# One list schedule for all engines in an attention + two-MLP kernel on one core

## The chip, the cores and the metric

One core of one Trainium2 chip. The metric is the device time of one execution in microseconds (us); lower is better. Three runs of the kernel before gave a median of 1007.41 us (1007.06 to 1010.12). The profile is of a further execution.

## What is computed

Three stages in a row, all float32 (cut from the reference):

```python
scores = (q @ k.T) / 8                      # 4 batches x 8 heads, 576 x 576, head 64
scores = where(scores >= max(scores) - tau, scores, -1e9)
x = softmax(scores) @ v                     # -> 2304 tokens x 512
h = x @ w_in                                # 512 -> 1024
s = h * softmax(h); x = layernorm(s) * g_ln @ w_out      # 1024 -> 512
h = x @ w2_in                               # 512 -> 2048
out = softplus(h) @ w2_out                  # 2048 -> 512
```

The weights arrive as 64-bit numbers, so the kernel turns each of them into float32 itself. Each MLP product is made of three matmuls in the fp32r format (high x high, high x low, low x high), for which every operand is split into a high part (a cast) and a low part (a subtraction).

## The kernel before

**Attention.** Two heads make a pair p (16 pairs), and an *item* is one pair with one or two tiles of 128 query rows, some with a *tail* (the last 64 rows of both heads). 36 items hold 80 score groups. `scores` (L177) multiplies the two heads on the two halves of TensorE's rows; VectorE takes the negated maximum (L187), ScalarE the exponential (L188), VectorE masks and sums (L195). The masked rows are transposed on TensorE through the identity (L210, L219, L221, L231), copied by ScalarE (L212, L224, L232), and multiplied with v (`av`, L276). `rinv`, `rgroup` and L279 bring in the reciprocal of the sums. Score tiles s take 4 of the 8 PSUM banks (one buffer for each head), everything else the 4 banks of the tag w.

**First MLP.** Nine *units* of 256 tokens. For each unit `m1_split` (L344, L345), `m1_h` (12 matmuls in a group, L355, 36 groups), `m1_post` (softmax, mean and variance on VectorE and ScalarE, L367 to L381), `m1_tr` (transposes L390, split L394, L395) and `m1_out` (24 matmuls in a group, L403, 36 groups). Its result x2 goes to DRAM (L407).

**Second MLP.** Five blocks, four of 512 tokens and one of 256, with 16 chunks of 128 hidden columns each. `m2_load` reads x2 back, `m2_split` splits it (ScalarE L541, GpSimd L542). For each chunk `m2_h` (12 matmuls, L573), softplus in nine steps of ScalarE and VectorE (L582 to L594), and `m2_y` (12 matmuls, L612; 6 in the last block).

**Weights.** `convert` makes float32 out of the two words of a weight (ScalarE L80, VectorE L81, L82, L84, ScalarE L87) and the low part (L88): on VectorE for the first MLP (8 pieces of 1024 columns), on GpSimd for the second (32 pieces of 512).

**The order of the work.** `attention` is a generator that yields after each half of a score group. The main loop at its foot gives the first MLP 0.6 of a step (PACE) for each step of attention, and advances the weight conversion at the steps listed in PREP. When attention is over, the rest of the first MLP runs with one conversion of w2_in between two of its steps; then the second MLP follows, with one conversion of w2_out for each chunk of its first block. The second MLP's work tiles lie in space that the first MLP gives back.

```python
493    for s, _ in enumerate(attention()):
494        if s in PREP:
495            next(prep, 0)
496        credit += PACE
497        while credit >= 1:
498            credit = credit - 1 if next(stream, False) else 0.0
```

Of the kernel before, what the change touches and what calls it, by code (L numbers as in the profile page):

```python
# [23 lines left out]
PACE = 0.6  # L24
PREP = [1, 2, 4, 5, 7, 8, 9, 11, *range(13, 37, 3)]
EB = 640

# [4 lines left out]

@with_exitstack
def tile_attention_solu_softplus(ctx: ExitStack, tc: tile.TileContext, q, k, v, tau, w_in, w_out, g_ln, w2_in, w2_out, out):
    nc = tc.nc
    PSUM = bass.MemoryType.PSUM
    pe, dve, act, pool, sp = nc.tensor, nc.vector, nc.scalar, nc.gpsimd, nc.sync
# [26 lines left out]
    items = [(b, h, ts, tail) for b, ts, tail in groups for h in range(NPAIR)]  # L64

    nw = [0]

    def bank():
        nw[0] += 1
        return psW.tile([P, 512], F32, tag="w", name=f"w{nw[0]}", bufs=4)  # L70

    w1h = w1.tile([P, 4, FF1], F32R, tag="w1h", name="w1h")
    w1l = w1.tile([P, 4, FF1], F32R, tag="w1l", name="w1l")
    wo1h = wo1.tile([P, 8, DM], F32R, tag="wo1h", name="wo1h")
    wo1l = wo1.tile([P, 8, DM], F32R, tag="wo1l", name="wo1l")

    def convert(raw, hi, lo, w_, post=None, sub=dve, view=lambda x: x):
        lw, hw = raw[:, :, 0], raw[:, :, 1]
        u = w_.bitcast(U32)
        act.activation(out=w_, in_=hw.bitcast(F32), func=AF.Abs, scale=2.0 ** -112)  # L80
        dve.tensor_scalar(out=lw, in0=lw, scalar1=29, scalar2=None, op0=ALU.logical_shift_right)  # L81
        dve.scalar_tensor_tensor(out=u, in0=u, scalar=3, in1=lw, op0=ALU.logical_shift_left, op1=ALU.bitwise_or)  # L82
        yield
        dve.scalar_tensor_tensor(out=u, in0=hw, scalar=0x80000000, in1=u, op0=ALU.bitwise_and, op1=ALU.bitwise_or)  # L84
        if post is not None:
            post(w_)
        act.copy(out=hi, in_=view(w_))  # L87
        sub.tensor_tensor(out=lo, in0=view(w_), in1=f(hi), op=ALU.subtract)  # L88
        yield

    def prep_w1():
        raws = {}

        def load(i):
            r = raws[i] = m1.tile([P, 1024, 2], U32, tag="lh" if i % 2 else "ll", name=f"raw1_{i}")
            c = 2 * (i % 2) if i < 4 else 2 * (i - 4)
            w = w_in[:, 512 * (i // 2):512 * (i // 2) + 512] if i < 4 else w_out
            sp.dma_start(out=r.rearrange("p (c n) t -> p c (n t)", c=2),
                         in_=w[c * P:(c + 2) * P, :].bitcast(U32).rearrange("(c p) e -> p c e", p=P))

        def two(x):
            return x.rearrange("p (c n) -> p c n", c=2)
        load(0)
        load(1)
        yield
        for i in range(8):
            w_ = m1.tile([P, 1024], F32, tag="u", name=f"w1_{i}", bufs=2)
            if i < 4:
                c, n = 2 * (i % 2), 512 * (i // 2)
                yield from convert(raws[i], w1h[:, c:c + 2, n:n + 512], w1l[:, c:c + 2, n:n + 512], w_, view=two)  # L110
            else:
                c = 2 * (i - 4)
                hi, lo = (w[:, c:c + 2, :].rearrange("p c e -> p (c e)") for w in (wo1h, wo1l))

                def post(w_, c=c):
                    for j in range(2):
                        wj = w_[:, j * DM:(j + 1) * DM]
                        dve.tensor_scalar_mul(wj, wj, g_sb[:, c + j:c + j + 1])
                yield from convert(raws[i], hi, lo, w_, post)
            if i + 2 < 8:  # L120
                load(i + 2)


    st = {}

    def load_qk(p):
        z = st[p] = {}
        z["q"] = at.tile([P, S], F32, tag="q", name=f"q{p}", bufs=NPAIR)
        z["k"] = at.tile([P, 640], F32, tag="k", name=f"k{p}", bufs=NPAIR)
        eng = act if p == 0 else sp  # L130
        for h in range(2):
            r = slice(64 * h, 64 * h + 64)
            sp.dma_start(out=z["k"][r, 0:576 + 64 * h], in_=k[p][:, 576 * h:576 + 640 * h])
            eng.dma_start(out=z["q"][r, :], in_=q[p][:, 640 * h:640 * h + 576])

    def load_v(p):
        z = st[p]
        z["v"] = at.tile([P, 640], F32, tag="v", name=f"v{p}", bufs=NPAIR)
        sp.dma_start(out=z["v"], in_=v[p])

    def scale_q(p):
        z = st[p]
        act.activation(out=z["q"], in_=z["q"], func=AF.Copy, scale=0.125)  # L143
# [4 lines left out]
    pend = []  # L148

    class Item:  # L150
        pass

    def begin(n):
        it = Item()
        it.n = n
        it.b, h, it.ts, it.tail = items[n]
        it.p = it.b * NPAIR + h
        it.h = h
        it.nt = len(it.ts)
        it.W = P * it.nt  # L160
        it.E = []
        it.e = {}
        it.sums = at.tile([P, 5], F32, tag="sums", name=f"sums{n}", bufs=3)
        it.rinv = at.tile([P, 5], F32, tag="rinv", name=f"rinv{n}", bufs=3)
        return it

    def scores(it, k_, apart):
        z = st[it.p]
        tail = k_ == it.nt
        i = 4 if tail else it.ts[k_]  # L170
        ps = [psS.tile([P, 2, 512], F32, tag=f"s{h}", name=f"s{it.n}_{k_}_{h}") for h in range(1 if tail else 2)]
        order = [(nh, h) for h in range(2) for nh in range(2)] if apart else [(nh, h) for nh in range(2) for h in range(2)]
        for nh, h in order:
            r, c, m = slice(64 * h, 64 * h + 64), qcol(h, i), 64 if tail else P
            kc = (64 if h == 1 and tail else 0) + 288 * nh
            o = ps[0][r, nh, 0:288] if tail else ps[h][:, nh, 0:288]
            pe.matmul(o, z["q"][r, c:c + m], z["k"][r, kc:kc + 288], start=True, stop=True)  # L177
        if tail:
            it.T = at.tile([P, 640], F32, tag="T", name=f"T{it.n}")
        else:  # L180
            it.E.append(at.tile([P, 1152], F32, tag="E", name=f"E{it.n}_{k_}", bufs=4))
        for h in range(len(ps)):
            s = 2 * k_ + h
            E = it.T[:, 0:576] if tail else it.E[k_][:, 576 * h:576 * h + 576]
            sv = ps[h][:, :, 0:288]
# [14 lines left out]
    def new_eT(it, what):  # L200
        return at.tile([P, 512], F32, tag="eT", name=f"eT{it.n}_{what}", bufs=NET)
# [281 lines left out]
    for p in range(NPAIR):  # L483
        scale_q(p)
# [206 lines left out]
```

## Time and profile before

| | |
|---|---|
| median of 3 runs | 1007.41 us |
| the profiled execution: time / span | 1010.33 us / 1008.5 us |
| TensorE busy / mean granted clock | 948.4 us (94%) / 0.971 |
| VectorE, ScalarE, GpSimd busy | 713.4, 568.9, 75.1 us |
| largest DMA user | q1, 53.99 MB, 17.1% of 16 engines |

Every engine works off its own queue in order, so an instruction that waits holds all that stand behind it on that engine. "Busy" is the time in which an instruction of the engine runs; matmuls overlap, and the granted clock of TensorE stands at 1.2 or 2.4 GHz, so busy time of TensorE is not work at full speed. The span runs from the first to the last instruction; the execution's time has 1.8 us more.

### The profile page before, as it was taken

How to read it: one execution, taken by the hardware profiler on the slowest of the kernel's cores; microseconds unless marked ns; L12 is line 12 of the kernel's file. 1: busy time of each engine (PE TensorE's matmuls, PEld its weight loads, DVE VectorE, ACT ScalarE, POOL GpSimd, SP SyncE). 2: the span in 40 equal slices, each digit the busy share in tenths (PEclk: the TensorE clock that was granted, in tenths of full speed). 3: DMA queues.
4: the chain of work that ended last, by engine and by line, in shares of the span. 5: the costliest groups of instructions: out<-in, count | busy, mean ns of one | idle time of the engine just before them, and what ended most of it. 6: DMA issues, size and time to landing. Idle time of an engine off the chain costs nothing.

```text
span 1008.5 us, 14610 instructions
## 1 busy us (share of the span) xinstructions
PE 948.4 (94%) x5664; PEld 747.2 (74%) x5664; DVE 713.4 (71%) x1387; ACT 568.9 (56%) x1082; POOL 75.1 (7%) x47
## 2 busy tenths in 40 slices
PE   3898999999999999999997699898999999999997
PEld 2666567777677777876886588676888788888896
DVE  5898866766768577676589959976555755665565
ACT  4765666666657567566556546544444444444453
POOL 0000000000000000000033534311001000000000
PEclk8898899999999999999998799998999999999999
DMA  8412200112001220000054533302000100100010
GB/s 220 173 61 79 75 27 12 35 44 78 27 11 36 65 69 15 12 11 6 33 162 141 162 127 103 125 1 84 1 0 22 63 1 1 42 1 0 1 44 21
DMA packets 27125, 55.21 MB, mean 55 GB/s; under 512 B 3248, under 2 KB 12464, under 8 KB 27056
## 3 DMA queue, kind: packets, MB, share of 16 engines
q1 hardware_dynamic: 26896, 53.99, 17.1%
q8 instruction: 44, 0.72, 0.3%
q10 hardware_dynamic: 160, 0.30, 0.1%
q14 instruction: 25, 0.20, 0.1%
HBM read 44.83 MB, written 9.44 MB: 54 GB/s over the span
## 4 chain that ended last, share of the span: by engine, by line
PE 67%; DVE 18%; ACT 8%; issue 3%; DMA 2%; SPq 0%; DVEq 0%; ACTq 0%
PE y L612 12%; PE h L573 12%; PE s L177 10%; PE w L355 9%; PE w L403 8%; PE w L276 7%; PE w L210 5%; DVE u L82 2%; DVE w L584 2%; DVE t L585 2%; DVE w L591 2%; DMA raw<-in_w_in_dram 2%; DVE u L84 2%; DVE w L592 1%; DVE gl L594 1%
## 5 line engine op out<-in xcount | busy, mean ns | idle before, releaser
L177 PE MATMUL s<-k,q 64*128 64x288 f32 (+1 forms) x640 | 135.0, 445 | 16.8 <-ACT q L143 8.9
L187 DVE TENSOR_REDUCE nm<-s 128x1 f32<-128x576 f32 x144 | 104.5, 750 | 43.4 <-PE s L177 43.4
L573 PE MATMUL h<-x2h,w2h 128*128 128x512 f32 (+1 forms) x320 | 119.3, 375 | 8.6 <-ACT x2h L541 7.0
L188 ACT ACTIVATE E<-s,nm 128x576 f32<-128x576 f32 x128 | 92.5, 741 | 52.6 <-DVE nm L187 52.4
L612 PE MATMUL y<-wo2h,gh 128*128 128x512 f32 x288 | 114.6, 398 | 7.5 <-ACT gh L593 4.3
L573 PE MATMUL h<-x2l,w2h 128*128 128x512 f32 (+1 forms) x320 | 118.8, 371 | 0.8 <-POOL x2l L542 0.8
L573 PE MATMUL h<-x2h,w2l 128*128 128x512 f32 (+1 forms) x320 | 118.6, 371 | 0.0
L612 PE MATMUL y<-wo2h,gl 128*128 128x512 f32 x288 | 113.8, 397 | 4.6 <-DVE gl L594 4.6
L612 PE MATMUL y<-wo2l,gh 128*128 128x512 f32 x288 | 113.4, 394 | 0.0
L195 DVE SCALAR_TENSOR_TENSOR E<-E,etau 128x576 f32<-128x576 f32 x128 | 102.5, 813 | 13.0 <-ACT E L188 9.1
L177 PEld LDWEIGHTS s<-k,q 64*128 64x128 f32 (+1 forms) x640 | 71.1, 182 | 53.8 <-issue 13.1
L586 ACT ACTIVATE w<-w 128x512 f32<-128x512 f32 (+1 forms) x80 | 47.1, 589 | 96.5 <-DVE t L585 96.4
L593 ACT CAST gh<-w 128x512 fp32r<-128x512 f32 (+1 forms) x80 | 46.2, 577 | 84.6 <-DVE w L592 84.3
L212 ACT COPY eT<-w 128x512 f32<-128x512 f32 x128 | 72.0, 592 | 24.2 <-PE w L210 23.7
L403 PE MATMUL w<-lh,wo1h 128*128 128x256 f32 x288 | 83.6, 291 | 0.0
L276 PE MATMUL w<-eT,v 128*64 128x256 f32 (+2 forms) x784 | 83.1, 357 | 0.0
L591 DVE SCALAR_TENSOR_TENSOR w<-h,w 128x512 f32<-128x512 f32 (+1 forms) x80 | 50.9, 637 | 44.7 <-ACT w L586 44.7
L403 PE MATMUL w<-ll,wo1h 128*128 128x256 f32 x288 | 81.5, 283 | 0.0
L403 PE MATMUL w<-lh,wo1l 128*128 128x256 f32 x288 | 81.4, 283 | 0.0
L594 DVE TENSOR_TENSOR gl<-w,gh 128x512 fp32r<-128x512 f32 (+1 forms) x80 | 51.0, 638 | 42.2 <-ACT gh L593 41.5
L276 PEld LDWEIGHTS w<-eT,v 128*64 128x64 f32 x784 | 52.8, 140 | 32.9 <-issue 9.7
L573 PEld LDWEIGHTS h<-x2h,w2h 128*128 128x128 f32 x320 | 61.4, 192 | 20.3 <-ACT x2h L541 7.2
(100 smaller groups left out, 1870.1 us busy)
## 6 DMA issues: line engine op xcount, KB each, us to landing
raw<-in_w_in_dram SPq DMA_DIRECT2D x16, 512.0 KB, 3.5
raw<-in_w_out_dram SPq DMA_DIRECT2D x16, 512.0 KB, 3.5
v<-in_v_dram SPq DMA_DIRECT2D x16, 320.0 KB, 3.0
x2s<-x SPq DMA_DIRECT2D x36, 128.0 KB, 1.7
x2r<-x2s SPq DMA_DIRECT2D x9, 512.0 KB, 4.0
q<-in_q_dram SPq DMA_DIRECT2D x30, 144.0 KB, 3.0
raw<-in_w_in_dram SPq DMA_DIRECT2D x4, 1024.0 KB, 8.9
raw<-in_w_out_dram SPq DMA_DIRECT2D x4, 1024.0 KB, 5.0
```

The lines of the kernel that those rows point to most:

```text
L177: pe.matmul(o, z["q"][r, c:c + m], z["k"][r, kc:kc + 288], start=True, stop=True)
L187: dve.tensor_reduce(out=nm, in_=sv, axis=AX.XY, op=ALU.max, negate=True)
L188: act.activation(out=E.rearrange("p (a b) -> p a b", a=2), in_=sv, func=AF.Exp, bias=nm, scale=1.0)
L195: dve.scalar_tensor_tensor(out=E, in0=E, scalar=etau, in1=E, op0=ALU.is_ge, op1=ALU.mult, accum_out=acc)
L212: act.copy(out=eT, in_=bk)
L276: pe.matmul(o[64 * h:64 * h + 64, :], w_, e, start=(i == 0), stop=(i == 4))
L355: pe.matmul(ps, x_[:, c, P * t:P * t + P], w_[:, c, 512 * n:512 * n + 512], start=(j == 0), stop=(j == 11))
L403: pe.matmul(o, w_[:, c, P * m:P * m + P], l_[:, c, :], start=(j == 0), stop=(j == 23))
L573: pe.matmul(ps, w_[:, kc, :], x_[:, kc, 0:n], start=(j == 0), stop=(j == 11))
L591: dve.scalar_tensor_tensor(out=w_, in0=ps, scalar=0.0, in1=w_, op0=ALU.max, op1=ALU.add)
L594: dve.tensor_tensor(out=gl, in0=w_, in1=f(gh), op=ALU.subtract)
L612: pe.matmul(y, g_[:, P * j:P * j + P], w_, start=(c == 0 and i == 0), stop=(c == NC2 - 1 and i == 2))
```

## The change

The program is written anew as a list of operations. Each states its engine, how long it occupies it (`occ`) and until its result is there (`fin`), what it comes after, which buffers it takes and uses, and a due number. `Plan.order` plays these through: at each step the engine that can start first takes, among what could start within 20 ns of that, the operation with the smallest due. The kernel emits all engines' instructions in that order and switches the framework's own reordering off (`manual_schedule`).

- An operation of attention is due at the number of its score group (0 to 79), a unit of the first MLP at its last group plus LAG = 100, the conversion of w2_in at 100 and up, of w2_out and the second MLP at 200 and up.
- The four matmuls of a score group are one operation that takes both score buffers; heads alternate.
- GpSimd makes the identity and nothing else: the low parts of the second MLP's weights (32 pieces) go to VectorE. `convert` works in place in the loaded words and has no tile of its own.
- `m1_out` makes x2 as high and low part (a cast of 256 columns, and 36 new subtractions on VectorE), stores 256 KB where it stored 128, and the second MLP loads both parts; the casts L541 and the subtractions L542 are gone.
- The second MLP's tiles and x2 buffers lie where the first MLP's w_in and the attention's x lay, and are opened as soon as these are done. Only w2_out and its conversion wait for the end of the first MLP.
- All loads are issued by SyncE, by due: q, k and v of batch 0 first, then the weights of the first MLP.

```diff
-PACE = 0.6
-PREP = [1, 2, 4, 5, 7, 8, 9, 11, *range(13, 37, 3)]
+LAG = 100
+PREP = [0, 1, 2, 3, 8, 9, 10, 11]
...
+            for e, c in cand.items():
+                got = []
+                for o in c:
+                    r = ready(o)
+                    if r is not None:
+                        got.append((max(r, free[e]), o))
+                if not got:
+                    continue
+                t = min(g[0] for g in got)
+                s, o = min((g for g in got if g[0] <= t + 20), key=lambda g: (g[1].due + (STICK if g[1].mode != mode and e == "PE" else 0), g[1].n))
+                if best is None or s < best[0]:
+                    best = s, o
...
+                for nh, h in ((0, 1), (0, 0), (1, 1), (1, 0)):
...
+            sc = op("PE", 970, 1128, emit_s, after=z["kq"] + [z["scaled"]], takes=s, uses=[z["q"], z["k"]], due=j, mode="Q" if is_t else "R")
...
+        a4 = op("DVE", 70 + 1068 * k_, 150 + 1070 * k_, lambda: dve.scalar_tensor_tensor(out=lw(), in0=hw(), scalar=3, in1=lw(), op0=ALU.logical_shift_left, op1=ALU.bitwise_or), after=[a1], uses=[raw], due=due)
...
+        return op("DVE", 70 + 1067 * k_, 150 + 1070 * k_, lambda: dve.tensor_tensor(out=lo(), in0=w_(), in1=f(hi()), op=ALU.subtract), after=[a5], uses=[raw], due=due)
...
+            b_ = op("DVE", 336, 420, lambda x2=x2, o=o: dve.tensor_tensor(out=x2.t[:, 1, :], in0=o.t[:, 0:256], in1=f(x2.t[:, 0, :]), op=ALU.subtract), after=[a], uses=[o, x2], due=d + 0.05 + 0.01 * m)
...
+    for u, un in enumerate(units):
+        m1_unit(u, max(last_tile[un, t] for t in range(2)) + LAG)
...
+        prep_w2("in", c, 100 + c, [o_w2a])
...
+    o_w2b = op("X", 0, 0, close_m1, behind=m1_ops + outs)
```

**VectorE at the start.** Before, from its third score maximum on (s: scores, E: exponentials, raw and w: a weight's words and result, rinv: reciprocals of the sums):

```order
L187 TENSOR_REDUCE nm_0_171<-s_0_0_164 128x1
L81 TENSOR_SCALAR raw_0_113<-raw_0_113 128x1024
L187 TENSOR_REDUCE nm_1_174<-s_0_1_165 128x1
L82 SCALAR_TENSOR_TENSOR w_0_158<-w_0_158,raw_0_113 128x1024
L238 TENSOR_SCALAR rinv_144<-sums_143 128x2
L195 SCALAR_TENSOR_TENSOR E_0_170,sums_162<-E_0_170,etau 128x576
L84 SCALAR_TENSOR_TENSOR w_0_158<-raw_0_113,w_0_158 128x1024
L239 RECIPROCAL rinv_144<-rinv_144 128x2
```

and after:

```order
L317 TENSOR_SCALAR rinv_232<-sums_216 128x2
L306 TENSOR_REDUCE nm_0_234<-s_0_0_218 128x1
L318 RECIPROCAL rinv_232<-rinv_232 128x2
L306 TENSOR_REDUCE nm_1_244<-s_0_1_219 128x1
L403 TENSOR_SCALAR raw_0_139<-raw_0_139 128x1024
L404 SCALAR_TENSOR_TENSOR raw_0_139<-raw_0_139 128x1024
L385 TENSOR_TENSOR xr_204<-w_260,x_253 128x128
L312 SCALAR_TENSOR_TENSOR E_0_258,sums_281<-E_0_258,etau 128x576 x2
```

The first conversion stood behind the third score maximum and ahead of the first reciprocal; now it stands behind the sixth maximum and the second reciprocal.

**TensorE at the end of the first MLP.** Before, from the last matmuls of unit 7 on (L403; ident transposes h of the last unit, L390; h_0, h_1, ...: chunks of the second MLP, L573):

```order
L403 MATMUL w_6012<-ll_5749,wo1h 128x256
L403 MATMUL w_6012<-lh_5748,wo1l 128x256
L390 MATMUL w_6042<-ident,h_0_5724 128x128 x4
L390 MATMUL w_6049<-ident,h_0_5724 128x128 x4
L573 MATMUL h_0_6239<-x2h_5974,w2h_5310 128x512
L573 MATMUL h_1_6270<-x2h_5974,w2h_5311 128x512
L573 MATMUL h_2_6309<-x2h_5974,w2h_5312 128x512
L573 MATMUL h_3_6360<-x2h_5974,w2h_5313 128x512
L573 MATMUL h_0_6239<-x2l_5975,w2h_5310 128x512
L390 MATMUL w_6056<-ident,h_1_5874 128x128 x4
```

and after (L453 is the last unit's h, L497 its transposes, L561 the second MLP's chunks, L514 the last unit's output):

```order
L453 MATMUL w_6019<-w1h,xl_1_5546 128x512
L497 MATMUL w_6053<-ident,h_0_5666 128x128 x4
L497 MATMUL w_6061<-ident,h_0_5666 128x128 x4
L561 MATMUL h_0_0_6094<-x2m_6043,w2h_4569 128x512 x2
L561 MATMUL h_0_0_6094<-x2m_6043,w2l_4570 128x512
L561 MATMUL h_0_0_6094<-x2m_6043,w2h_4569 128x512 x2
L561 MATMUL h_0_0_6094<-x2m_6043,w2l_4570 128x512
L497 MATMUL w_6102<-ident,h_1_5865 128x128 x4
L497 MATMUL w_6107<-ident,h_1_5865 128x128 x4
L561 MATMUL h_0_0_6094<-x2m_6043,w2h_4569 128x512 x2
```

Before, the matmuls of the second MLP that stood ahead of the first MLP's last one were ten, of four chunks mixed; now they are 24, two whole chunks, set between the transposes and the output groups. In the whole order, behind the last matmul of attention and up to the last of the first MLP, there stood 96 of the 432 matmuls L355, 48 of the 144 L390 and 312 of the 864 L403 before; after the change there stand 243, 96 and 576 of the same.

## Rows read from the trace of the kernel before

**Rows 1.** the page, part 1: busy us, share of the span, instructions, of each engine.

```profile
PE 948.4 (94%) x5664; PEld 747.2 (74%) x5664; DVE 713.4 (71%) x1387; ACT 568.9 (56%) x1082; POOL 75.1 (7%) x47
```

**Rows 2.** busy by stretch: the stretch, its us, busy us (instructions) by engine, PEclk, DMA share, GB/s.

```profile
0.00:30.00 30.00, 14.80 (x66) 10.46 (x66) 17.60 (x31) 15.23 (x25) 0.70 (x6) 0.83 0.89 240
30.00:150.00 120.00, 110.63 (x730) 75.57 (x731) 101.03 (x219) 80.47 (x153) 0.00 (x0) 0.91 0.23 73
150.00:500.00 350.00, 347.82 (x2586) 266.34 (x2585) 243.21 (x570) 219.63 (x444) 0.00 (x0) 1.00 0.10 31
500.00:580.00 80.00, 64.21 (x390) 56.33 (x387) 68.63 (x116) 47.43 (x92) 31.43 (x19) 0.89 0.48 154
580.00:700.00 120.00, 110.91 (x502) 88.32 (x500) 94.27 (x134) 62.74 (x110) 35.80 (x20) 0.98 0.26 88
700.00:1008.50 308.50, 300.07 (x1398) 250.16 (x1398) 188.68 (x320) 143.45 (x260) 7.19 (x3) 0.99 0.05 18
```

**Rows 3.** pieces of the chain of waits: start, us, engine, tile, line, instructions in the piece.

```profile
150.62 2.31 PE w L276 x20
...
153.30 2.75 PE w L355 x12
...
158.25 2.89 PE w L403 x24
...
202.29 1.75 PE w L390 x16
...
259.15 2.89 PE w L276 x40
...
709.48 2.72 PE h L573 x12
...
712.20 2.72 PE y L612 x12
...
976.89 1.43 PE h L573 x12
```

**Rows 4.** timeline of TensorE, 300 to 317 us: start, us, instruction, how many.

```profile
300.48 1.24 PE L177 MATMUL s<-k,q 64*128 64x288 f32 x8
301.65 2.38 PE L276 MATMUL w<-eT,v 128*64 128x256 f32 x20
...
314.68 1.97 PE L177 MATMUL s<-k,q 64*128 64x288 f32 x8
316.58 2.38 PE L276 MATMUL w<-eT,v 128*64 128x256 f32 x20
```

**Rows 5.** VectorE: timeline at 151 us; all maxima, ns min/median/max, first and last start.

```profile
151.27 1.41 DVE L187 TENSOR_REDUCE nm<-s 128x1 f32<-128x576 f32 x2
...
L187 DVE TENSOR_REDUCE nm<-s x144: 715/750/761, 8.2 to 486.8; 128x1 f32<-128x576 f32 x144
```

**Rows 6.** waits, 0 to 150 us (first two) and 500 to 720 us: total, times, longest.

```profile
PE s L177 <- ACT q L143: 8.9, 3, 5.9
...
PE w L250 <- ACT rb L245: 8.3, 4, 6.3
...
PE h L573 <- ACT x2h L541: 7.0, 1, 7.0
...
PE w L390 <- DVE h L381: 6.9, 2, 5.9
...
DVE w L584 <- DMA x2s<-x: 9.1, 1, 9.1
```

**Rows 7.** timeline of the SyncE queue at the start.

```profile
0.73 1.47 SPq L133 DMA_DIRECT2D k<-in_k_dram  x2
```

**Rows 8.** three lines from 500 us on: duration ns min/median/max, first and last start.

```profile
L82 DVE SCALAR_TENSOR_TENSOR u<-u,raw x32: 676/694/2897, 507.9 to 658.8; 128x512 uint32<-128x512 uint32 x32
L84 DVE SCALAR_TENSOR_TENSOR u<-raw,u x32: 668/680/1765, 509.1 to 660.4; 128x512 uint32<-128x512 uint32 x32
L88 POOL TENSOR_TENSOR wo2l<-u,wo2h x16: 1276/1354/3554, 592.1 to 661.9; 128x512 fp32r<-128x512 f32 x16
```

More of the change, by code (lines that the diff above doesn't have):

```diff
@@ L77, in convert @@
[L77 to L121, printed above, removed]
@@ L131, in load_qk @@
         for h in range(2):
             r = slice(64 * h, 64 * h + 64)
[L133 to L143, printed above, removed]
+            z["kq"].append(load("SP", lambda r=r, h=h: k_.t[r, 0:576 + 64 * h], lambda h=h: k[p][:, 576 * h:576 + 640 * h], 150, takes=[k_] if h == 0 else (), uses=[k_] if h else (), due=due, after=behind))
@@ new lines, in load_qk, with load_v @@
+        ql = []
+        for h in range(2):
+            r = slice(64 * h, 64 * h + 64)
+            ql.append(load("SP", lambda r=r: q_.t[r, :], lambda h=h: q[p][:, 640 * h:640 * h + 576], 144, takes=[q_] if h == 0 else (), uses=[q_] if h else (), due=due, after=behind))
+        z["scaled"] = op("ACT", 574, 678, lambda: act.activation(out=q_.t, in_=q_.t, func=AF.Copy, scale=0.125), after=ql, uses=[q_], due=due + 0.5)
+    def load_v(p, due, behind=()):
+        v_ = st[p]["v"] = buf("at", "v", f"v{p}", [P, 640], bufs=NPAIR)
+        st[p]["vl"] = load("SP", lambda: v_.t, lambda: v[p], 320, takes=[v_], due=due, after=behind)
@@ L167, in scores @@
[L167 to L185, printed above, removed]
-            nm = at.tile([P, 1], F32, tag="nm", name=f"nm{it.n}_{s}", bufs=4)
-            dve.tensor_reduce(out=nm, in_=sv, axis=AX.XY, op=ALU.max, negate=True)
-            act.activation(out=E.rearrange("p (a b) -> p a b", a=2), in_=sv, func=AF.Exp, bias=nm, scale=1.0)
-            pend.append((E, it.sums[:, s:s + 1]))
-        return len(ps)
@@ new lines, in m2_chunk, with emit @@
+        ps = buf("psH", "h2", f"h2_{bi}_{c}", [P, 512], bufs=4)
+        prev = None
+        for part in range(4):
+            def emit(part=part):
+                for j_, (a, b_) in enumerate((("h", 0), ("h", 1), ("l", 0))):
+                    pe.matmul(ps.t[:, 0:n], w2t["in", a, c][:, part, :], x.t[:, b_, part, 0:n], start=(part == 0 and j_ == 0), stop=(part == 3 and j_ == 2))
+            oc = 681 if n == 512 else 360
+            prev = op("PE", oc, oc + 170, emit, after=xl_[bi] + [wready["2in", c]] + ([prev] if prev else []), takes=[ps] if part == 0 else (), uses=[x] + ([] if part == 0 else [ps]), due=due + 0.001 * part, mode="F")
@@ new lines, in plan_of @@
+    load_v(0, -45)
+    load_qk(2, -44)
+    load_qk(3, -42)
+    for p in range(1, NPAIR):
+        load_v(p, -41 + p)
+    first_tile = {}
+    n_tile = 0
+    for n, (b, h_, ts, tail) in enumerate(items):
+        first_tile.setdefault(b * NPAIR + h_, n_tile)
+        n_tile += len(ts) + tail
+    for i in range(8):
+        prep_w1(i, PREP[i])
+    last_tile = {}
+    for n, (b, h_, ts, tail) in enumerate(items):
+        p = b * NPAIR + h_
+        if b and p not in st:
+            load_qk(p, first_tile[p] - 6)
+            load_v(p, first_tile[p] - 5)
+        item(n)
+        for t in ts:
+            last_tile[(b, ts[0] // 2), t % 2] = tile_no[0]
+        if tail:
+            last_tile["T", b // 2] = tile_no[0]
```

870 lines of the change are left out of this document (454 added, 416 removed).

## The prediction, made before any run of the changed kernel

> **What bounds the kernel now.** I read the page's busy times first, then the stretches, then the chain of waits for what a piece of work takes at full clock, and last the waits of the two stretches that lose time. The page says TensorE: 94% busy, every other engine under three quarters [rows 1]. The stretches say where it is not: TensorE idles 15.2 us in the first 30, 9.4 up to 150, 2.2 from there to 500, 15.8 from 500 to 580, 9.1 up to 700, 8.4 in the rest, 60.1 us in all [rows 2]. They also give the granted clock: 0.83, 0.91, 1.00, 0.89, 0.98, 0.99, which over those lengths is 5.1 + 10.8 + 0 + 8.8 + 2.4 + 3.1 = 30 us of full-speed time not granted; every loss of clock lies in or beside a stretch with idle time.
>
> Next, the work itself at full clock. The chain gives 2.75 us for 12 matmuls of h (L355), 2.89 for 24 of the first MLP's output, 1.75 for 16 transposes, 2.31 for an item's product with v and 2.89 with a tail, 2.72 for a chunk of either product of the second MLP and 1.43 for the small block's h [rows 3]. A score group of four matmuls (eight records) takes 1.17 us to the start of the next instruction when its two heads run side by side, and 1.90 when they don't [rows 4]. So: scores 80 x 1.17 = 94; transposes 720 x 1.75/16 = 79; products with v 28 x 2.31 + 8 x 1.16 (half, an estimate) + 16 x 0.58 = 83; first MLP 36 x 2.75 + 9 x 1.75 + 36 x 2.89 = 219; second 64 x (2.72 + 2.72) + 16 x (1.43 + 1.36) = 393. The sum is **868 us**. The span of 1008.5 is thus 868 of work + 60 idle + 30 of missing clock + some 50 of changing between kinds of matmul and of slower score groups. By the busy row alone only 60 us could be won; by this sum it is 140.
>
> The Trainium skill (Perfetto Trace Analysis, Identifying the Most-Contended Engine) says the same against the page: TensorE's matmul busy share is a poor measure of the distance to its roof. [...]
>
> **The change, part by part.** The matmuls and transposes are the same in number, and the printed order changes from one kind to another about as often (some 480 runs of one kind against 500), so neither the 868 nor most of the 50 moves. What can move are the idle time, the clock that goes with it, and the score groups.
>
> *The start.* Until its 45th score maximum, which the kernel before runs at 152 us [rows 5], VectorE is the fuller engine: it was busy 17.6 + 101.0 us of the first 150 [rows 2]. Its work up to that maximum is the same in the new order: 44 maxima, 44 masks, all eight conversions of the first MLP, two softmax steps, about 118 us by the same durations; TensorE's, by the pieces above, about 90. So the start can't end before 8 + 118 = 126 us, which is the gain's upper bound, 26 us. What stood in the way was order: TensorE waited 8.9 us for scaled q and 8.3 for the copy of the reciprocals (6.3 of it once) [rows 6], while VectorE's first reciprocal stood behind a conversion and the third item's q was loaded behind 2 MB of weights. In the new order six maxima go ahead of the first conversion. Against it: the two loads of the first q go to SyncE's queue behind two of k, and each such issue takes 0.73 us [rows 7], so they go out 1.5 us later; and the first weights now wait for 3.7 MB of q, k and v. At the 240 GB/s of the first 30 us [rows 2] the first MB of weights is there at about 4.7/0.24 + 1 = 21 us, when VectorE has only some 8 + 8 us of its own work ahead: up to 5 us of waiting, with the third item's masks queued behind it. I take **-10 us** (VectorE 88% full, 82% before); the ends are -26 and +5.
>
> *Score groups.* Eleven groups took 1.85 to 2.01 us, such as the one at 314.68 [rows 4]. As one operation with alternating heads, begun when both buffers are planned free, most run side by side: 11 x 0.73 = 8; I take **-6**, between -12 and 0, for a head whose buffer comes late still runs alone.
>
> *From attention's end on.* Here TensorE lost 33.3 us idle and 14.3 of clock [rows 2]. It waited 6.9 us for the last unit's normalised h and 7.0 for the split of x2 [rows 6], and VectorE, in front of both, was held up: the same 512-column operation takes 0.69 us in the median and up to 2.90, and GpSimd's subtraction 1.28 to 3.55 [rows 8]. The long ones stand beside GpSimd's. Taking GpSimd out removes this; the 32 subtractions at 0.68 (the like operation L84) put 22 us on VectorE [rows 8], and the 36 small ones, half as wide, 24 at the most. I cost both at nothing: they lie beside 140 and 87 us of TensorE work (below) in which VectorE has room. The cover is thinnest in the first block of the second MLP: there VectorE has nine operations for each chunk, at most 0.60 from one start to the next (0.68 less the 0.08 or so that the next one overlaps, as the two maxima of 0.75 that take 1.41 [rows 5]), 5.4 us, and TensorE 5.44. If it goes, 16 chunks lose about 0.5 each, 8 us. The wait of 9.1 us for x2's store [rows 6] goes, since the second MLP's tiles no longer lie where x2 was, and so does the 7.0: x2 comes split. What is late next is the first w2_out piece, converted only after the first MLP; in front of it stand two to three chunks of h, 6 to 8 us, and its chain of six operations at 0.6 to 0.7 takes about 4.5.
>
> Against that, more of the first MLP now runs without attention beside it: 243 matmuls, 96 transposes and 576 matmuls, 20.25 x 2.75 + 6 x 1.75 + 24 x 2.89 = 136 us, with 5 us of the second MLP as filling, where it was about 67. There each unit must go through the chain of maximum, exponential, product, square, normalisation and transposes with three buffers for h and one for its transposed form. I allow 12 us idle and 7 of clock for that and the change of stage, 3 for the first w2_out piece, and leave the last stretch's 8.4 and its 3.1. That is 23.4 + 10.1 = 33.5 in place of 47.6: **-14**; the ends are -36 (only the last stretch's losses stay) and +30 (below).
>
> *DMA.* x2 costs 128 KB more at each of 36 stores and as much on reading, about 9 MB over 500 us at DMA shares of 0.05 to 0.26 [rows 2]; hidden.
>
> **The sum:** 1008.5 - 10 - 6 - 14 = 978.5 of span. The profiled execution took 1010.3, 2.9 above the median of 1007.4; counted from the median, -30 us gives 977. I predict **977 us**.
>
> **The rivals.**
>
> *A: the first MLP alone is as gappy as 500 to 580 us was* (slower). There 80 us held 64.2 busy at clock 0.89, 55.4 us of full-speed work [rows 2]: 1.44 us for each. The 141 us of work after attention would take 203 in place of the 160 that I allow with 19 us of idle time and clock: +43, so 1020. It decides from a loss of 49 us in that stage on, 0.35 for each us of work. For it: the chain through VectorE and ScalarE is the same, and the conversions of w2_in are due before most units there, so they go ahead of the chain. Against it: in the old stretch the chain was held by VectorE operations of up to 2.9 us beside GpSimd [rows 8], and only two units were left to fill each other's gaps; now more than five are, and chunks of the second MLP stand in the last ones. The Trainium skill (TensorE: Matmul & The Clock Gate, Why this matters for your kernels) warns of idle gaps between bursts of matmuls, since the clock then falls; the trace agrees, with 0.89 in the gappiest stretch and 1.00 in the fullest [rows 2].
>
> *B: attention's own circle sets its pace* (no change). Two score buffers mean: scores, maximum, exponential, then the next scores. Before, the maxima of the 80 groups ran from 8.2 to 486.8 us [rows 5], 6.0 us for a group. In my sum they end near 400, 4.9 each. If VectorE and ScalarE serve the circle late and it takes 5.3 to 5.4, the gain is eaten: 80 x 0.4 = 32, so about 1009. For it: on VectorE conversions and softmax steps of 1.1 us stand in the circle's way. Against it: from 150 to 500 us VectorE was busy only 243 of 350 us and ScalarE 220 [rows 2], so the circle had room there and was not what set the pace.
>
> *C: GpSimd's work is missed* (a smaller gain). VectorE becomes the bound in the first block of the second MLP and at the change of stage: +8, and the 3 us there doubled: 988.
>
> *D: all of it works* (a larger gain). VectorE full from the start and no gap in the middle: 1007 - 22 - 8 - 30 = 947.
>
> **How the numbers follow.** The forecast with its bounds, D among it, 0.68; A 0.15; B 0.12; C 0.05. A measurement of this kernel tells about 0.3%, 3 us, from no change. The forecast and C lie below that; of A 0.13 above and 0.02 within; of B 0.04 below, 0.06 within, 0.02 above. So faster 0.77, same 0.08, slower 0.15. The range goes from D's 947 to 1015; above it lies some two thirds of A, 0.1, and below it a few hundredths.
>
> **What would show it.** Right: the 45th maximum at about 142 us; attention's last score group between 390 and 410; no VectorE operation of 512 columns above 0.75 us from there on; TensorE's idle time near 42 us and a mean clock of 0.98; the second MLP 395 to 405 us long, as now. Wrong: attention's end above 430 (B), a stretch of over 180 us from there to the last first-MLP output (A), or TensorE waiting for VectorE in the first block of the second MLP for more than 10 us (C). If TensorE's idle time stays at 60 us although attention ends early, the gain has been handed back in the stage behind it.

## The result and the profile after

The kernel after takes a median of 976.25 us (975.49 to 978.67, 4 runs); beside it the kernel before took 1008.3 (1007.06 to 1010.12, 4 runs). The ratio is 0.9685, 95% interval 0.9661 to 0.9709. The forecast was 977. Medians and ratios here and below are of fast runs; one execution, of x3_heads_apart at 1025.1 us, fell in a slower state and is left out.

The page's busy row, and the costliest group of score matmuls, of the kernel after:

```profile
PE 919.7 (94%) x5664; PEld 735.8 (75%) x5664; DVE 703.9 (72%) x1455; ACT 564.2 (58%) x1073; POOL 0.7 (0%) x6
...
L295 PE MATMUL s<-k,q 64*128 64x288 f32 (+1 forms) x640 | 114.7, 455 | 14.8 <-ACT q L245 6.5
```

TensorE's share is what it was in [rows 1], 94%, of a span 31.6 us shorter. Its busy time fell by 28.7 us with the same matmuls; its idle time only from 60.1 to 57.2.

The two kernels cut at the same four events (the 45th score maximum, the last one, the end of the last first-MLP output, the end), as busy time by stretch; columns: stretch, us, busy us (instructions) of PE, PEld, DVE, ACT, POOL, granted clock, DMA share, GB/s. Before:

```profile
0.00:151.30 151.30, 126.74 (x804) 86.73 (x806) 119.93 (x253) 96.30 (x179) 0.70 (x6) 0.90 0.36 106
151.30:486.80 335.50, 333.32 (x2477) 254.78 (x2474) 234.37 (x548) 209.04 (x420) 0.00 (x0) 1.00 0.11 32
486.80:590.30 103.50, 87.71 (x577) 77.49 (x575) 80.45 (x140) 59.59 (x118) 34.19 (x20) 0.92 0.43 139
590.30:1008.50 418.20, 400.67 (x1814) 328.18 (x1813) 278.67 (x449) 204.02 (x365) 40.24 (x22) 0.99 0.10 34
```

and after:

```profile
0.00:150.30 150.30, 117.02 (x811) 81.83 (x812) 119.97 (x252) 95.39 (x177) 0.70 (x6) 0.89 0.34 106
150.30:409.50 259.20, 257.29 (x2054) 189.87 (x2054) 201.96 (x472) 173.56 (x350) 0.00 (x0) 1.00 0.13 41
409.50:582.10 172.60, 156.49 (x1003) 139.97 (x1002) 117.34 (x271) 95.25 (x192) 0.00 (x0) 0.95 0.36 116
582.10:976.90 394.80, 388.90 (x1800) 324.12 (x1799) 264.61 (x465) 200.02 (x354) 0.00 (x0) 1.00 0.14 45
```

In the kernel after, the row of VectorE's timeline that sets the first cut, and all its score maxima with their first and last start (before: [rows 5]):

```profile
150.30 0.75 DVE L306 TENSOR_REDUCE nm<-s 128x1 f32<-128x576 f32 x1
```

```profile
L306 DVE TENSOR_REDUCE nm<-s x144: 717/751/760, 8.8 to 409.5; 128x1 f32<-128x576 f32 x144
```

In each stretch I subtract the work at full clock (the instructions of each kind in it, at the prediction's pitches from [rows 3, 4]) from its length; what remains is loss: idle time, missing clock, and matmuls that ran one by one where they could have overlapped.

| | length before, after | work before, after | loss before, after |
|---|---|---|---|
| to the 45th maximum | 151.3, 150.3 | 87.6, 86.9 | 63.7, 63.4 |
| to the last maximum | 335.5, 259.2 | 309.5, 244.3 | 26.0, 14.9 |
| to the last first-MLP output | 103.5, 172.6 | 80.7, 149.4 | 22.8, 23.2 |
| second MLP | 418.2, 394.8 | 390.6, 387.5 | 27.6, 7.3 |
| sum | 1008.5, 976.9 | 868, 868 | 140, 109 |

So the 31 us come from two places: 20 from the second MLP, 11 from attention behind its 45th maximum. The start gave nothing, and the first MLP alone, 69 us longer, lost no more than the shorter stretch before. (The work to the 45th maximum holds the prediction's estimate for the small items' product with v, in both kernels alike.)

The 11 us of attention are the score matmuls' own. Their busy time in that stretch, 440 records in both kernels (columns: PE, PEld, granted clock, DMA share, GB/s), before and after:

```profile
151.30:486.80 335.50, 82.85 (x440) 43.54 (x440) 1.00 0.11 32
```

```profile
150.30:409.50 259.20, 71.32 (x440) 38.22 (x440) 1.00 0.13 41
```

What TensorE waited for in the kernel after (total us, times, longest), which answers to [rows 6]:

```profile
PE h L561 <- DMA x2m<-x2s: 8.6, 2, 7.9
PE w L330 <- ACT rb L324: 7.6, 5, 2.5
...
PE s L295 <- ACT q L245: 6.5, 1, 6.5
PE s L295 <- ACT E L308: 6.0, 3, 3.2
PE w L497 <- DVE h L484: 5.1, 2, 2.8
PE w L584 <- ACT gh L579: 2.0, 2, 1.3
```

and the chain of waits at the change of stage (start, us, what):

```profile
553.36 8.53 DMA x2m<-x2s
...
562.02 2.47 PE h L561 x5
```

The 7.0 us for the split of x2 are gone, but the second MLP's first chunk now waits 7.9 us at once for x2 itself, whose load could be issued only when the first MLP's last h was done. VectorE's operations of 512 columns (ns min/median/max) answer to [rows 8]:

```profile
L404 DVE SCALAR_TENSOR_TENSOR raw_in<-raw_in x16: 680/687/695, 423.1 to 492.4; 128x512 uint32<-128x512 uint32 x16
L578 DVE TENSOR_TENSOR gw<-gw,t x80: 417/691/693, 571.7 to 970.5; 128x512 f32<-128x512 f32 x64, 128x256 f32<-128x256 f32 x16
```

None is above 0.70 us now; [rows 8] showed up to 2.90.

### The profile page after: what moved, and what is told of

Its sections match the earlier page's. It is cut to its first block, busy times and chain, and to the rows that moved or that the text cites. A ratio compares the mean times of both kernels' runs of the same rounds, so it can differ in the third digit from the quotient of the medians.

```text
span 976.9 us, 14613 instructions
## 1 busy us (share of the span) xinstructions
PE 919.7 (94%) x5664; PEld 735.8 (75%) x5664; DVE 703.9 (72%) x1455; ACT 564.2 (58%) x1073; POOL 0.7 (0%) x6
## 4 chain that ended last, share of the span: by engine, by line
PE 80%; DVE 8%; DMA 4%; ACT 3%; SPq 2%; issue 2%; DVEq 0%; ACTq 0%
PE h L561 20%; PE w L584 20%; PE s L295 9%; PE w L514 8%; PE w L382 8%; PE w L453 7%; PE w L345 6%; SPq L227 2%; DMA q<-in_q_dram 2%; DMA raw_in<-in_w_in_dram 1%; PE w L497 1%; DMA x2m<-x2s 1%; DVE nm L306 1%; ACT E L308 1%; DVE E L312 1%
## 5 line engine op out<-in xcount | busy, mean ns | idle before, releaser
L561 PE MATMUL h<-x2m,w2h 128*128 128x512 f32 (+1 forms) x640 | 183.1, 370 | 8.6 <-DMA x2m<-x2s 8.6
L561 PEld LDWEIGHTS h<-x2m,w2h 128*128 128x128 f32 x640 | 117.6, 190 | 30.3 <-issue 9.3
L561 PE MATMUL h<-x2m,w2l 128*128 128x512 f32 (+1 forms) x320 | 118.2, 369 | 0.0
L584 PE MATMUL w<-wo2h,gh 128*128 128x512 f32 x288 | 112.7, 391 | 2.0 <-ACT gh L579 2.0
L584 PE MATMUL w<-wo2l,gh 128*128 128x512 f32 x288 | 112.2, 390 | 0.0
L584 PE MATMUL w<-wo2h,gl 128*128 128x512 f32 x288 | 112.1, 389 | 0.0
L348 ACT COPY eT<-w 128x512 f32<-128x512 f32 (+2 forms) x164 | 82.6, 557 | 39.7 <-PE w L345 39.2
L514 PE MATMUL w<-lh,wo1h 128*128 128x256 f32 x288 | 83.9, 291 | 0.0
L345 PE MATMUL w<-ident,E 128*128 128x128 f32 x576 | 81.2, 288 | 0.5 <-DVE ll L504 0.2
L514 PE MATMUL w<-lh,wo1l 128*128 128x256 f32 x288 | 81.4, 283 | 0.0
L514 PE MATMUL w<-ll,wo1h 128*128 128x256 f32 x288 | 81.4, 283 | 0.0
L345 PEld LDWEIGHTS w<-ident,E 128*128 128x128 f32 x576 | 66.8, 147 | 18.3 <-issue 6.7
L577 DVE SCALAR_TENSOR_TENSOR gw<-h,gw 128x512 f32<-128x512 f32 (+1 forms) x80 | 50.9, 637 | 38.3 <-ACT gw L576 37.5
```

What stands on the lines that cost most here:

```text
L345: pe.transpose(bk.t[:, P * i:P * i + P], b_.t[:, c:c + P], ident)
L348: copies.append(op("ACT", occ, occ + 111, lambda: act.copy(out=eT.t[:, 0:width], in_=bk.t[:, 0:width]), after=[g], uses=[bk, eT], due=due))
L514: pe.matmul(o.t[:, 0:256], w_[:, c, P * m:P * m + P], l_[:, c, :], start=(c == 0 and j_ == 0), stop=(c == 7 and j_ == 2))
L561: pe.matmul(ps.t[:, 0:n], w2t["in", a, c][:, part, :], x.t[:, b_, part, 0:n], start=(part == 0 and j_ == 0), stop=(part == 3 and j_ == 2))
L577: a6 = V(lambda: dve.scalar_tensor_tensor(out=v(w_), in0=v(ps), scalar=0.0, in1=v(w_), op0=ALU.max, op1=ALU.add), [a5], (), [ps, w_])
L584: pe.matmul(ys[j].t, g_.t[:, P * j:P * j + P], w2t["out", a, c], start=(c == 0 and i == 0), stop=(c == NC2 - 1 and i == 2))
```

## The experiments

Each kernel was timed in three rounds beside the kernel before. The stage ends in the text are the same events as above.

### GpSimd alone, both ways

Kernel x2_before_no_gpsimd is the kernel before with VectorE in GpSimd's place, with no other edit:

```diff
-            for _ in convert(raws[c], hi[c], lo[c], w_, sub=pool):
+            for _ in convert(raws[c], hi[c], lo[c], w_, sub=dve):
...
-        pool.tensor_tensor(out=xl, in0=xr2, in1=f(xh), op=ALU.subtract)
+        dve.tensor_tensor(out=xl, in0=xr2, in1=f(xh), op=ALU.subtract)
```

> The kernel before, with all 32 low parts of the second MLP's weights and the nine low parts of x2 on VectorE in place of GpSimd; nothing else. Theory G: the second MLP is 10 to 20 us shorter than 418, the time 988 to 998. Rival O: within 4 us of 1008, since what stood there was the order in which the queues were written.

Kernel x1_gpsimd_low is the kernel after with 32 subtractions handed back:

```diff
+        if n == 512:
+            return op("POOL", 1250, 1400, lambda: pool.tensor_tensor(out=lo(), in0=w_(), in1=f(hi()), op=ALU.subtract), after=[a5], uses=[raw], due=due)
         return op("DVE", 70 + 1067 * k_, 150 + 1070 * k_, lambda: dve.tensor_tensor(out=lo(), ...
```

> The kernel after, with the low parts of the second MLP's 32 weight pieces back on GpSimd (VectorE has 32 subtractions, some 20 us, less). Theory G (GpSimd's long operations hold VectorE up, and that cost the kernel before most of its loss in the second MLP): VectorE's 512-column operations of 0.69 us go above 1.5 us beside them, the second MLP's length goes from 395 us back towards 405 to 415, and the time is 986 to 998. Rival O (the second MLP gained by the new order and the earlier tiles): the time stays at 973 to 980, whatever single VectorE operations do.

Measured: x2_before_no_gpsimd 985.96 us (ratio 0.9764, 0.9747 to 0.9782), 23.7 below the kernel before beside it (1009.6) and a little past theory G's 988. x1_gpsimd_low 989.98 (0.9827, 0.9791 to 0.9863), 13.7 above the kernel after. Theory G holds in both, and rival O, which takes the order for the cause, falls in both. The queues did not stay wholly as they were, for the framework ordered them anew in x2_before_no_gpsimd and the plan in x1_gpsimd_low; but of TensorE's 5664 matmuls all but 51 in the one and 224 in the other stand in the old sequence. The kernel before's L584, and in x2_before_no_gpsimd two of VectorE's operations and the last two stages:

```profile
L584 DVE TENSOR_SCALAR w<-t x80: 284/427/2248, 596.6 to 1000.5; 128x512 f32<-128x512 f32 x64, 128x256 f32<-128x256 f32 x16
```

```profile
L82 DVE SCALAR_TENSOR_TENSOR u<-u,raw x32: 678/685/695, 506.2 to 651.6; 128x512 uint32<-128x512 uint32 x32
L584 DVE TENSOR_SCALAR w<-t x80: 283/426/430, 587.7 to 975.3; 128x512 f32<-128x512 f32 x64, 128x256 f32<-128x256 f32 x16
```

```profile
485.10:583.60 98.50, 85.20 (x569) 76.00 (x567) 76.36 (x160) 59.81 (x118) 0.00 (x0) 0.93 0.46 146
583.60:983.40 399.80, 393.77 (x1822) 328.44 (x1821) 271.44 (x470) 204.74 (x365) 0.00 (x0) 1.00 0.11 35
```

L82 no longer exceeds 0.70 us and L584, which took up to 2.25 us in the kernel before, 0.43. The second MLP takes 399.8 in place of 418.2 us, the stage ahead of it 98.5 in place of 103.5, attention ends at 485.1 in place of 486.8: the gain lies where GpSimd worked. (The matmuls that changed places lie between 512 and 614 us, so a part of the 5 us ahead of the second MLP can be order.) By the measure of the table the second MLP loses about 8 us here, as in the kernel after: GpSimd alone accounts for that stage's 20. And these two edited lines bring the kernel before to within 10 us of the kernel after. In x1_gpsimd_low VectorE's long operations are back, and TensorE waits for what hangs on them. Operations, the last two stages, TensorE's waits:

```profile
L404 DVE SCALAR_TENSOR_TENSOR raw_in<-raw_in x16: 676/694/1805, 420.4 to 501.1; 128x512 uint32<-128x512 uint32 x16
L580 DVE TENSOR_TENSOR gw<-gw,t x80: 417/691/1802, 573.4 to 980.1; 128x512 f32<-128x512 f32 x64, 128x256 f32<-128x256 f32 x16
```

```profile
406.80:583.70 176.90, 156.52 (x1003) 139.60 (x1002) 120.87 (x255) 94.11 (x192) 23.43 (x16) 0.95 0.34 113
583.70:986.50 402.80, 391.89 (x1801) 323.57 (x1799) 267.94 (x449) 200.96 (x354) 23.53 (x16) 1.00 0.13 44
```

```profile
PE w L499 <- DVE h L486: 11.2, 3, 7.7
...
PE w L586 <- DVE gl L582: 2.6, 4, 1.2
```

In the kernel after the wait for h was 5.1 us, and that for gl does not appear. VectorE had 32 subtractions less to do, and the last two stages took 4.3 and 8.0 us more. What one such collision costs is seen in the kernel before, at 690 us, in the timelines of GpSimd, of VectorE and of TensorE (in brackets: idle before, and what ended it):

```profile
690.58 2.39 POOL L542 TENSOR_TENSOR x2l<-x2r,x2h 128x1024 fp32r<-128x1024 f32 x1 [5.29 <-ACT x2h L541]
```

```profile
691.07 2.19 DVE L584 TENSOR_SCALAR w<-t 128x512 f32<-128x512 f32 x1 [1.27 <-ACT t L583]
```

```profile
692.03 0.39 PE L612 MATMUL y<-wo2h,gl 128*128 128x512 f32 x1
...
696.84 0.47 PE L612 MATMUL y<-wo2h,gh 128*128 128x512 f32 x1 [1.71 <-ACT gh L593]
...
697.53 0.70 PE L612 MATMUL y<-wo2h,gl 128*128 128x512 f32 x1
```

GpSimd's subtraction of 1024 columns begins at 690.58 and ends at 692.97. VectorE's L584, 0.43 us in the median, begins 0.49 after it and ends 0.29 after it: 2.19 us. From there the softplus chain is late (a part of the lateness is ScalarE's cast of x2, L541, 1.04 us, which runs ahead of L583), TensorE idles 1.71 us, and the third matmul behind the gap takes 0.70, where the same kind took 0.39 at 692.03: the granted clock behind the gap is half, the lower of its two levels (1.2 and 2.4 GHz), as this stretch shows:

```profile
697.50:704.00 6.50, 5.43 (x13) 3.83 (x13) 4.61 (x8) 3.52 (x7) 0.00 (x0) 0.51 0.44 161
```

Here lateness costs the gap and then the clock. GpSimd suffers too: its subtraction took 1.28 at the least and up to 3.55 [rows 8].

The Trainium skill (SBUF — State Buffer, Who interferes with whom) has this as an exclusive lock of a port pair, held for a whole instruction, by VectorE operations with two SBUF inputs or in a two-port mode against GpSimd; the rows above agree in that L584, 0.43 us by itself, does not end before GpSimd's subtraction has ended; what was held meanwhile no row shows.

### The two heads of a score group apart

```diff
-            sc = op("PE", 970, 1128, emit_s, after=z["kq"] + [z["scaled"]], takes=s, ...
+                scs = [op("PE", 850, 1010, lambda h=h, e=emit_h: e(h), after=z["kq"] + [z["scaled"]], takes=[s[h]], ...) for h in range(2)]
```

> The kernel after, with the four matmuls of a score group as two operations, one head after the other, each begun when its own buffer is free. 72 groups cost 1.90 in place of 1.17 us on TensorE. If TensorE sets the pace in all of attention: 72 x 0.73 = 53 us longer, about 1029. If VectorE sets it up to the 45th maximum and TensorE behind it: some 32 groups x 0.73 = 23, about 999. If the earlier start of the first head gives the time back (its maximum can run 0.5 us sooner): 976 to 984.

Measured: 1016.84 us (1009.8 to 1023.8 in nine runs; ratio 1.0078, 1.0051 to 1.0105), 41 above the kernel after, between the first two expectations. (The 72 groups of the expectation are 64: of the 80, 16 are tails, which the edit leaves as they were.) Its profile is of the shortest run:

```profile
142.50:448.80 306.30, 303.19 (x2132) 217.96 (x2131) 214.82 (x504) 187.84 (x372) 0.00 (x0) 1.00 0.12 36
448.80:612.90 164.10, 150.11 (x983) 134.83 (x984) 116.29 (x267) 93.24 (x190) 0.00 (x0) 0.97 0.37 121
```

The 45th maximum came at 142.5 us, 8 earlier than in the kernel after (a first head's maximum does run sooner), and the last at 448.8, 39 later; 8 us came back in the stage behind. So behind the start TensorE sets attention's pace and the groups pay for their order; the start came no later for it.

### How far attention goes first

The only edit is LAG, 100 in the kernel after: 0 in x4_lag0, 30 in x8_lag30.

> The kernel after with LAG = 0 in place of 100: a unit of the first MLP is due as soon as its last score group is, so attention no longer goes first. Theory F (attention first is worth something, since the end of attention comes 70 us later otherwise and only few units are left to fill each other's gaps): attention's last maximum at 450 to 490, 990 to 1005. Rival N (what fills TensorE is the list schedule, in whatever order): 972 to 982. Rival H (the first MLP alone lost 23 us after attention, which it wouldn't beside attention): 960 to 970.

> The kernel after with LAG = 30: a unit of the first MLP is due 30 score groups behind its last one. LAG 100 gave 976, LAG 0 gave 1069. If the loss grows with every unit that is served beside attention (attention's circle is broken by long matmul groups): 1000 to 1030, attention's last maximum at 450 to 500. If only a fully mixed order breaks the circle, and units beside attention save the loss of the stage behind it: 965 to 978.

Measured: x4_lag0 1068.84 us (1.0594, 1.0553 to 1.0636), far outside all that I expected; x8_lag30 969.78 (0.961, 0.9587 to 0.9632), 6.5 below the kernel after. In x4_lag0, TensorE's two longest waits, the stretch from the 45th maximum to the last, and one step of the conversions of w2_in and w2_out (first and last start):

```profile
PE s L295 <- ACT E L308: 25.3, 20, 3.5
PE w L584 <- ACT wo2h L410: 23.3, 1, 23.3
```

```profile
177.60:592.00 414.40, 371.38 (x2685) 291.94 (x2685) 252.78 (x598) 222.36 (x445) 0.00 (x0) 0.95 0.11 37
```

```profile
L404 DVE SCALAR_TENSOR_TENSOR raw_in<-raw_in x16: 676/686/694, 603.2 to 677.6; 128x512 uint32<-128x512 uint32 x16
L404 DVE SCALAR_TENSOR_TENSOR raw_out<-raw_out x16: 678/684/696, 681.5 to 757.4; 128x512 uint32<-128x512 uint32 x16
```

With LAG 0 a unit that has become ready is due ahead of all attention that is left: the first MLP first, not an even mixture. Attention's circle (scores, maximum, exponential, transposes) then starves: TensorE idles 43 us from the 45th to the last maximum, which comes at 592 us, and early in the second MLP it waits 23.3 us at once for the first w2_out piece. That piece's conversion stands behind the 16 of w2_in, which need the space that attention gives back: they begin at 603 us, with the first MLP nearly done, where in the kernel after they began at 423 and ran beside it. With LAG 30, from attention's last maximum to the first MLP's last output:

```profile
442.10:572.80 130.70, 119.42 (x788) 107.50 (x787) 97.45 (x221) 75.94 (x154) 0.00 (x0) 0.96 0.41 143
```

Attention ends 33 us later than in the kernel after, and the first MLP alone is 42 us shorter and idles 11.3 us in place of 16.1. Going strictly first is not needed; what must not happen is that the first MLP goes ahead.

### The start

x5_dma_model gives the plan the trace's numbers for loads; x6_prep_fill gives the conversions of the first MLP's weights later due numbers, so that on VectorE they yield to what attention has ready.

```diff
-                dma = max(dma, s + 600) + o.kb * 1024 / 330
+                dma = max(dma, s + 600) + o.kb * 1024 / 240
...
-        return op(eng, 60, None, lambda: e.dma_start(out=out(), in_=in_()), ...
+        return op(eng, 600, None, lambda: e.dma_start(out=out(), in_=in_()), ...
```

> The kernel after with two numbers of the plan set to what its trace shows: an issue occupies a queue for 600 ns (planned 60) and data flow at 240 GB/s (planned 330). Nothing else is touched, so only the orders move: the scaling of the fourth q now stands behind the first exponentials on ScalarE, and the second MLP's first chunk in front of the last transposes goes behind them. Theory L (the start was slow since ScalarE's queue stood in front of exponentials at loads that the plan believed to be there): the 45th maximum comes 5 to 10 us before 146, the wait of 8.6 us for x2m falls below 6, the time is 964 to 972. Rival V (VectorE's own 116 us of work set the start): within 3 us of 976.

```diff
-PREP = [0, 1, 2, 3, 8, 9, 10, 11]
+PREP = [40, 41, 42, 43, 44, 45, 46, 47]
```

> The kernel after with the eight conversions of the first MLP's weights due at 40 to 47 in place of 0 to 11, so that on VectorE they only fill what attention leaves. Theory V (VectorE sets the start, and what it does there beyond attention costs as much): of the 35 us of conversions some 15 move behind the 45th maximum, which comes at 125 to 135, and since TensorE lost 63 us up to there, the time is 962 to 970. Rival W (TensorE then lacks the first MLP's work as filling, or the stage behind is longer by as much): 973 to 980.

(The 146 us of these expectations are where the 43rd maximum stood; counted out, the 45th of the kernel after is at 150.3.) Measured: x5_dma_model 968.98 us (0.9597, 0.9578 to 0.9617), 7 below the kernel after, but not for theory L's reason: the 45th maximum came at 151.0. The wait for x2m left TensorE's list, and one of another kind grew from 5.1 us to what follows. The profile is of the slowest of five runs, 973.7 us, so where the 7 us of the median lie is not shown.

```profile
PE w L497 <- DVE h L484: 16.7, 3, 7.6
```

x6_prep_fill took 958.99 (0.9508, 0.9489 to 0.9527), 17 below the kernel after, below theory V's range but on its side. Its two stages of attention, and the last step of the conversions there and in the kernel after (first and last start):

```profile
0.00:136.00 136.00, 111.74 (x801) 76.37 (x802) 114.93 (x236) 92.22 (x170) 0.70 (x6) 0.94 0.38 118
136.00:393.40 257.40, 255.64 (x2079) 190.53 (x2080) 206.26 (x487) 177.16 (x358) 0.00 (x0) 1.00 0.14 43
```

```profile
L411 DVE TENSOR_TENSOR wo1l<-raw,wo1h x4: 1216/1226/1226, 75.9 to 122.0; 128x1024 fp32r<-128x1024 f32 x4
```

```profile
L411 DVE TENSOR_TENSOR wo1l<-raw,wo1h x4: 1215/1218/1222, 68.2 to 98.1; 128x1024 fp32r<-128x1024 f32 x4
```

The 45th maximum came at 136.0, 14 us earlier, and nothing was paid back: the next stretch took 257.4 in place of 259.2. The 15 us of moved conversions were wrong: all eight still run ahead of the 45th maximum, the last of them ending at 123 in place of 99 us. The 5 us of VectorE's work that left that stretch (114.9 against 120.0) are other operations of the first MLP, and the wait for q is still 6.3. The edit changes only orders; what went, as I read it, is conversions of 1.2 us standing in front of maxima and masks that were ready in VectorE's queue. TensorE's idle time up to there fell from 33.3 to 24.3 us, and with it the missing clock, from 16.5 to 8.2 (0.89 and 0.94 of the two stretches).

### The change of stage

x9_out_later is x5_dma_model with the first MLP's outputs (and their cast and subtraction) due 8 later; y4_out_only has that without the loads' numbers.

```diff
-                prev = op("PE", 720, 885, emit, ..., due=d + 0.05 + 0.01 * m + 0.001 * part, mode="F")
+                prev = op("PE", 720, 885, emit, ..., due=d + 8 + 0.05 + 0.01 * m + 0.001 * part, mode="F")
```

> The kernel of x5_dma_model with the first MLP's output matmuls (24 in a group) due 8 later, so that TensorE takes the next units' h first and outputs of two units are left as filling at the change of stage. If the idle time in the first MLP alone is the wait for the last units' softmax and transposes: that stage loses 8 to 12 us in place of 23, and the time is 6 to 12 us below x5_dma_model. If the stage is bound by VectorE's and ScalarE's chain through one lh and ll buffer: within 3 us of x5_dma_model.

> The kernel after with the first MLP's outputs due 8 later and nothing else (the plan's numbers for loads as they were). x5_dma_model was 7 us below the kernel after, x9_out_later 14 below x5_dma_model. If the two are independent: 960 to 964. If the right numbers are what lets the fillers stand in the right place: 966 to 974.

Measured: x9_out_later 954.72 us (0.9461, 0.9438 to 0.9485), 14 below x5_dma_model; y4_out_only 974.23 (0.9665, 0.9638 to 0.9692), only 2 below the kernel after, at the end of its second expectation. In x9_out_later, first MLP alone and second MLP:

```profile
403.20:567.20 164.00, 160.03 (x1037) 142.60 (x1034) 124.51 (x284) 99.17 (x202) 0.00 (x0) 0.99 0.37 121
567.20:952.80 385.60, 379.73 (x1761) 316.96 (x1760) 254.47 (x451) 193.90 (x344) 0.00 (x0) 1.00 0.14 46
```

TensorE idles 4.0 us in the first in place of 16.1, at clock 0.99, and the second MLP's own stretch holds 39 matmuls less than in the kernel after (1761 in place of 1800), since they fill the stage ahead of it. In x9_out_later no wait for the last units' h above 0.2 us is left. In y4_out_only the same due brought the wait for x2m from 8.6 to 2.7 us, but left this one:

```profile
PE w L497 <- DVE h L484: 7.0, 1, 7.0
```

and attention ended 5 us later: its stretch holds 24 matmuls of the first MLP's h (156 in place of 132) and 12 of its outputs more, about 6 us of work, at the same loss as in the kernel after. So the due and the durations of loads give 21 us together, and 2 and 7 by themselves; the runs show which waits were left, but not why the two need each other.

### All together

y1_all is x9_out_later with x6_prep_fill's due numbers, y2_all_lag30 the same with LAG 30.

> The kernel of x9_out_later with the eight conversions due at 40 to 47 as in x6_prep_fill. If the two gains lie in different stages, they add: x6_prep_fill was 17 us below the kernel after, x9_out_later 21, so 934 to 942. If x6_prep_fill moved work into the stage that x9_out_later filled: 946 to 955.

> The kernel of y1_all with LAG = 30. LAG 30 alone gave 6 to 7 us, all of it behind attention, where 131 in place of 173 us of first MLP stood alone. If that stage has lost its idle time in y1_all already: within 3 us of y1_all. If each gain is of its own: 5 to 7 us below y1_all.

y1_all took 945.54 us (0.9381, 0.9366 to 0.9397), 31 below the kernel after and the fastest of all; between the two expectations, so the gains add but for 8 us: the start and the first MLP alone are as short as in the run that each gain comes from, or shorter, but attention behind the start takes 261.5 us, where x6_prep_fill has 257.4. y2_all_lag30 took 948.59 (0.9411, 0.9387 to 0.9434): LAG 30 gives nothing once the stage behind attention is full. The first three stages of y1_all:

```profile
0.00:132.80 132.80, 107.71 (x789) 75.08 (x790) 111.96 (x228) 90.64 (x167) 0.70 (x6) 0.94 0.38 120
132.80:394.30 261.50, 260.34 (x2081) 195.78 (x2083) 207.95 (x495) 177.98 (x361) 0.00 (x0) 0.99 0.14 42
394.30:556.50 162.20, 158.40 (x1037) 141.41 (x1034) 124.53 (x284) 99.19 (x202) 0.00 (x0) 1.00 0.37 122
```

## Why the prediction was right, and where it was not

The total was right to 1 us by luck: errors of the terms cancelled. The step that failed is "neither the 868 nor most of the 50 moves". The prediction looked for its gain in idle time and clock, to 42 us and 0.98. But of the 31.6 us of span idle time gave 2.9, and the clock, 0.971 and 0.973 in the mean, about 3. Some 26 came out of those 50, the changing between kinds of matmul and the slower score groups: 11 in attention behind the start, 10 in the start, where idle time grew by 9 and took them back, and 4 in the second MLP.

- **The start, -10: failed.** It gave 1.0 us. The step that failed is "VectorE 88% full": its work was the same 120 us, but in 150.3 us, 80%. I took an order with six maxima ahead of the first conversion for the cure, but the conversions behind it, due at 1 to 11, still went ahead of maxima that were due later. Due behind them (x6_prep_fill), the same eight run in the same stretch and the start is 14 us shorter, inside the bound of 26.
- **Score groups, -6: right in kind, too small.** The stretch behind the start lost 11 us less, and the busy time of its score matmuls fell by as much, from 82.9 to 71.3; x3_heads_apart shows that their order is paid for there. The eleven slow groups of 1.85 to 2.01 us became five of 1.86, which is some 4 us. The prediction missed the rest: nine more groups of the kernel before were cut by other matmuls (at 257 us two, two of another kind, then six), and none of the kernel after is.
- **From attention's end, -14: right in mechanism and nearly in size, wrong in place.** The loss went from 50.4 to 30.5, -20; idle time and clock alone, which the term counts, from about 47 to 31, -16. I split it into 12 + 7 us for the first MLP alone, which lost 23, and "leave the last stretch's 8.4 and its 3.1", which failed: the second MLP fell from 27.6 to 7.3. I had counted there idle time and clock by two stretches, 580 to 700 and the rest [rows 2], 23 us in all, and missed that its length was 418 us against 391 of work, and that most of those 23 were GpSimd's doing; "395 to 405 us long, as now" misread the kernel before. GpSimd's removal, which I named for this stage and did not price by itself, is the largest single term: 23.7 us taken alone in the kernel before, and 13.7 when 32 subtractions are handed back in the kernel after. The 3 us for the first w2_out piece do not appear: TensorE has no wait for it.
- **GpSimd's work on VectorE at nothing: right.** In the second MLP TensorE's waits for other engines come to 2.0 us in all; x1_gpsimd_low, with VectorE freed of the 32 subtractions, is slower. Rival C did not happen.
- **x2's transfers hidden: failed in one place.** The loads of both parts end the wait of 8.6 us at the change of stage, where before there was 7.0 for the split.
- **Rival A** asked for a stretch above 180 us: it was 172.6. **Rival B** asked for attention's end above 430: it was 409.5, inside 390 to 410. Idle time was forecast at 42 us and clock at 0.98; they were 57 and 0.973, since the start kept its losses. **Rival D**'s 947 was reached only with three more sets of edits (y1_all, 945.5).

## What to carry to other kernels

Measure a stage's loss as its length less its work at full clock, not as idle time: the second MLP hid 28 us of loss behind a TensorE that was busy 401 of 418 us. An engine that looks free is not free if its operations hold up another one's: GpSimd was busy 7% of the time and taking it out was worth 23.7 us alone, where the whole rewriting gave 32. A list schedule is only as good as its durations and its priorities: two durations of loads and two sets of due numbers were worth another 31 us.

## What the runs showed that I had not expected

- A GpSimd subtraction and a VectorE operation delay each other: L584 goes from 0.43 to as much as 2.25 us, GpSimd's own from 1.28 to 3.55. Giving 47 us of GpSimd's time back cost 14 us (x1_gpsimd_low).
- Due numbers alone, with the same instructions on every engine, moved the time by 93 us one way (x4_lag0) and 17 the other (x6_prep_fill).
- The two heads' matmuls one after the other cost 41 us over 64 groups, 0.64 each, less than the 0.73 seen in single groups [rows 4].
